# RWKV-7 attention and a SoLU block: couplings with 33 weight columns from chunk 12 on, the second block's inverse loaded into place, the first coupling ahead of two waves of h

## The chip, the cores and the metric

The kernel runs on one core of a Trainium2 chip. The time is device microseconds of one execution, the median of several runs. An engine has its own instruction queue: PE (TensorE) multiplies matrices into PSUM, PEld is its loading of weights, DVE (VectorE) and ACT (ScalarE) work on tiles, POOL (GpSimd) does a little arithmetic and issues DMAs, SP issues DMAs only. A queue runs in order, so an instruction that waits holds up everything behind it on its engine.

## The reference

Two blocks in a row. The first is a recurrence over 768 steps for 4 batches of 8 heads, with a state of 40 x 40 each:

```python
for t in range(S):
    y[:, :, t] = np.einsum('bhd,bhde->bhe', rt, state)
    Sa = np.einsum('bhde,bhe->bhd', state, at)
    state_decay = state * wt[:, :, None, :] - np.einsum('bhd,bhe->bhde', Sa, bt)
    state = state_decay + np.einsum('bhd,bhe->bhde', vt, kt)
```

Its output, as 3072 tokens of 320, goes through the second: h = x @ w_in (320 to 1024), e = exp(h - max), solu = h * e / sum(e), a normalization over the 1024 columns, and a product with w_out back to 320.

## The kernel before, in words

The 768 steps are cut into chunks of C = 64 tokens, and two batches share the 128 partitions, so there are 24 pieces of work (12 chunks of the sequence for 2 pairs of batches), called chunk 0 to 23 below. Within a chunk the recurrence becomes matrix products, with one triangular system of 64 unknowns for each of 16 pairs of batch and head. The inverse of its matrix is made in blocks of Q = 32: DVE inverts the two 32 x 32 diagonal blocks, for two chunks at once (`invert`, L543), and SP stores them to DRAM as `uu_dram` (`unloaded`, L566). `bring` (L573) loads them back in two shapes: the first block into `tu`, columns Q to 2Q, the second into the lower rows of `uh`. Then two couplings on PE make the block below the diagonal, and put it beside the second block:

- `flip` (L586), on DVE, transposes the first block inside `tu`.
- `couple` (L592), the first coupling: 16 matmuls of `nt` (weights, 64 rows x 64 columns) with the flipped first block (32 moving columns), into the PSUM tile `py`. ACT copies the result to `wy` (L602), times a mask `hi` that clears the upper 32 rows of each half. The right half of `wy` holds a constant, the identity in the lower rows.
- `close` (L605), the second coupling: 16 matmuls of `wy` (64 x 64) with `uh` (32 moving columns). The product gives the block below the diagonal in the upper rows, and, through the identity in `wy`, the second block itself in the lower rows. ACT copies all of it to the last third of `tu` (L614), "tu's tail" below.
- `solved` (L730), a step of the loop later, multiplies `tu` with `x0`.

The 16 matmuls of a coupling take turns over four tiles of 64 x 64 of the array (`in_turn`, L309); `mm` is the helper at L317, so that all of them carry the line L318. The weights' columns become the result's partitions.

The main loop (L1149) runs over i. Step i works on several chunks at once: it prepares chunk i + 5, couples chunk i + 1, solves chunk i, and does the second block's h for chunk c = i - 2. The second block's product h is cut into five waves (`hidden`, L814; 18 matmuls of 512 moving columns and 4 of 256 in all), and `run` (L1236) places them between the other PE work by the table `waves` (L1233): from i = 5 to 22 two go at place 2, one at place 3, one at place 6 (L1293), just ahead of the first coupling, and one at place 7 (L1298), between the two couplings. The second coupling is at L1300, `driven` (`px<-lv,psi`) at L1303.

Every operation is recorded under a name by `do` and then emitted in the order of the list `ORDER` (L31); names that the list does not hold follow in the order in which they were recorded. The list ends with the work around the coupling of chunk 10, so from chunk 11 on the loop's own order stands. At the end of step i the queues get, in this order: `rs` (POOL, L871), the loads of `tu` and `uh` for chunk i + 2 (`bring_`, L1338; SP), the stores of x for chunk i (`leave`, L796; POOL, three DMAs, read back by SP at L812 as `xT`), and at the start of an odd step the load of r for a later chunk (L371; POOL), which ACT copies in the same step (`by_value`, L379). In even steps the inverse of the next two chunks has been stored (L570, SP) just before.

Of the kernel before, what the change touches and what calls it, by code (L numbers as in the profile page):

```python
# [13 lines left out]
AF = mybir.ActivationFunctionType  # L14
# [3 lines left out]
P = 128  # L18
C = 64
Q = 32  # L20
# [7 lines left out]
SPLITS = {2: (0, 0, 0, 2, 4), 24: (0, 0, 0, 0, 2)}  # L28


ORDER = """  # L31
w0 b0 b1 w1 a0 lg0 Tc0 xi0 xe0 Tei0 sb0 Tb0 Ta0 L1 lg1 Tc1 Eei0 Ea0 v0 Eb0 xi1 xe1 N0 nt0 Tei1 Eei1 sb1 Tb1 a1 Ta1 Ea1
L0 Eb1 N1 nt1 w2 lg2 a2 Tc2 nb0 k0 Z0 sn0 nb1 ns1 nf1 sn1q sk0 ns0 nf0 sn1 w3 xe2 b2 Z1 Ta2 xi2 B0 Tei2 Eei2 r0 Ea2
# [65 lines left out]
def kernel(  # L99
# [18 lines left out]
    nc = tc.nc  # L118
    B, H, S, D = r.shape
# [24 lines left out]
    def c_(name):  # L144
        lo, hi = where[name]
        return cst[:, lo:hi]
# [22 lines left out]
    for x in ex_t:  # L169
# [8 lines left out]
    wy = const.tile([P, 2, 4, C], FP32, name="wy")  # L178
    nc.vector.tensor_copy(out=wy.rearrange("p h j c -> p (h j) c")[:, :, Q:],
                          in_=c_("eye_hi").unsqueeze(1).to_broadcast([P, 8, Q]))  # L180
# [114 lines left out]
    def centred(mean):  # L295
        for x in range(0, NF, NF // 2):
            nc.vector.tensor_tensor(out=w2[:, x:x + NF // 2], in0=w2[:, x:x + NF // 2],
                                    in1=mean.unsqueeze(1).to_broadcast([P, NF // 2, DM]), op=ALU.subtract)


    def half(p):
        return slice(C * p, C * p + C)
# [6 lines left out]
    def in_turn(tile_of, some=units):  # L309

        lots = {}
        for u in some:
            lots.setdefault(tile_of(*u), []).append(u)
        lots = list(lots.values())
        return [lot[n] for n in range(max(map(len, lots))) for lot in lots if n < len(lot)]

    def mm(o, lhsT, rhs, start=True, stop=True):  # L317
        nc.tensor.matmul(o, lhsT=lhsT, rhs=rhs, start=start, stop=stop, skip_group_check=True)  # L318
# [28 lines left out]
    def ok(i):  # L347
        return 0 <= i < N
# [145 lines left out]
    def shared_pair(i):  # L494

        if i not in shared:
            shared[i] = pair(st[i]["Y"], "py")
        return shared[i]
# [74 lines left out]
    def bring(i, which):  # L573
        if not ok(i):
            return
        d = st[i]
        d["tu"], d["uh"] = tu_t[i % 2], uh_t[i % 2]
        n, at = divmod(i, GRP)
        src = inverse[n].rearrange("c (e a x h) t -> e a c x h t", e=2, a=GRP, x=2)
        for x in range(2 * (which == "t")):  # L580
            queue = nc.sync if i or not x else nc.gpsimd
            queue.dma_start(out=d["tu"][C * x:C * x + Q, :, Q:2 * Q], in_=src[0, at, :, x])
        for x in range(2 * (which == "u")):
            nc.sync.dma_start(out=d["uh"][C * x + Q:C * x + C], in_=src[1, at].rearrange("c x h t -> c (x h) t"))

    def flip(i):  # L586
        if not ok(i):
# [4 lines left out]
    def couple(i):  # L592
        if not ok(i):
            return lambda: None
        d = st[i]
        t = shared_pair(i)
        for u in in_turn(lambda p, q, g, h: (p ^ h, p)):
            p, q, g, h = u
            j = 2 * q + g
            x = half(p ^ h)  # L600
            mm(t[half(p), h, j * Q:j * Q + Q], d["nt"][x, p, j], d["tu"][x, 4 * p + j, 0:Q])
        return lambda: nc.scalar.activation(out=wy[:, :, :, 0:Q], in_=t[:, :, 0:4 * Q].rearrange("p h (j c) -> p h j c", j=4),  # L602
                             func=AF.Copy, scale=c_("hi"))

    def close(i):  # L605
        if not ok(i):
            return lambda: None
        d = st[i]
        t = shared_pair(i)
        for u in in_turn(lambda p, q, g, h: (p, p ^ h)):  # L610
            p, q, g, h = u
            j = 2 * q + g
            mm(t[half(p ^ h), p, 384 + j * Q:384 + j * Q + Q], wy[half(p), h, j], d["uh"][half(p), H * (p ^ h) + 4 * p + j])
        return lambda: nc.scalar.copy(out=d["tu"].rearrange("p (h j) c -> p h j c", h=2)[:, :, :, 2 * Q:],  # L614
                       in_=t[:, :, 384:].rearrange("p h (j c) -> p h j c", j=4))


    def attend_kv(i, t, which):
# [322 lines left out]
    def do(name, fn, *args):  # L941
        seq.append((name, lambda: fn(*args)))

    def do_pe(name, fn):
        box = []
        do(name, lambda: box.append(fn()))
        return box
# [25 lines left out]
    def vector(plan, i=None):  # L973
        for word in plan.split():
            if word in "bsf":
                stage = "bsf".index(word)
                x = begun[stage]
                begun[stage] += 1
                do(f"n{word}{x}", narrowed, x, stage)
                if stage == 2 and x in LANDS_NEXT:  # L980
                    do(f"L{LANDS_NEXT[x]}", land, LANDS_NEXT[x], nc.gpsimd)
            else:
                some(int(word.strip("o")), (i + 2) // GRP if "o" in word else N)
# [29 lines left out]
    def evict(name, box, *which):  # L1013
        if which:
            do(name, lambda: [box[0][x]() for x in which])
        else:
            do(name, lambda: box[0]())
# [22 lines left out]
    def bring_(i):  # L1040
        if ok(i):
            do(f"tu{i}", bring, i, "t")
            do(f"uh{i}", bring, i, "u")

    def xy(i):
        return "BC" if i < EARLY - AHEAD else ("BC", "CB")[(i - EARLY + AHEAD) % 2]
# [89 lines left out]
    reads(1)  # L1136
    scaled_(4, "k")
    bring_(0)
    bring_(1)
    do("L3", land, 3, nc.sync)  # L1140
    keys(5, "k")
# [7 lines left out]
    for i in range(-1, N + LAG + 1):  # L1149
        j, c = i + AHEAD, i - LAG  # L1150
# [85 lines left out]
        def run(x):  # L1236
            if not ok(c):
                return
            for _ in range(waves[x]):
                n = next(wave)  # L1240
                do(f"H{c}.{n}", hidden, c, n)
            if sum(waves[:x + 1]) == NK and sum(waves[:x]) < NK:
                do(f"m{c}", highest, c)
# [46 lines left out]
        ahead = 2 + (i >= EARLY - AHEAD)  # L1290
        logged_(j + ahead)
        vector(plan[2], i)
        run(6)  # L1293
        if ok(i + 1):
            evict(f"wy{i + 1}", do_pe(f"C{i + 1}", lambda i=i: couple(i + 1)))
        if i == LAG + 1:
            do("centre", lambda: centred(mean["mean2"]))
        run(7)  # L1298
        if ok(i + 1):
            evict(f"tl{i + 1}", do_pe(f"D{i + 1}", lambda i=i: close(i + 1)))  # L1300
# [31 lines left out]
        if i >= 0:  # L1332
            some(Q, (i + 2) // GRP)
            odd = steady and i % GRP == 1
            if odd:
                keys(j + 2, "k")
                keys(j + 4, "w")
            bring_(i + 2)  # L1338
            if odd:
                keys(j + 3, "ak")  # L1340
                keys(j + 5, "w")
# [21 lines left out]

    place = {name: x for x, name in enumerate(ORDER.split())}
    for name, piece in sorted(seq, key=lambda x: place.get(x[0], len(place))):
# [31 lines left out]
```

## Time and profile before

| what | value |
|---|---|
| median of 3 runs | 532.44 us (528.31 to 536.37) |
| the profiled execution | 535.16 us, span 533.3 us |
| mean granted TensorE clock | 0.990 |
| PE busy | 487.6 us, 91% of the span |
| DVE, ACT, POOL busy | 420.0, 313.1, 180.2 us |
| first and last coupling | 60.5 us, 486.7 us |

The span is from the first to the last instruction of the program. Lines of the profile are read as: source line, engine, operation, output<-inputs, for matmuls "rows*columns" of weights and the shape of the moving operand, and xN for the number of records. A matmul in fp32 is recorded as two passes, so 16 matmuls are x32. "SPq" is SP's queue of DMA issues. Where a wait is given, it reads "idle time <- what ended it".

### The profile page before, as it was taken

The page shows a single profiled execution, that of the slowest core. Times are in us where ns is not written, and L with a number is a line of the kernel's source. Part 1 is how long each engine was busy: PE and PEld are TensorE (multiplying, and loading weights), DVE is VectorE, ACT ScalarE, POOL GpSimd, SP SyncE. Part 2 cuts the span into 40 slices and gives each one's busy share as a digit, 9 for nine tenths or more (in the row PEclk, how much of TensorE's full clock was granted, in tenths as well). Part 3 has the DMA queues.
Part 4 walks back from the last instruction along what each step waited for, and adds up shares of the span by engine and source line. Part 5 has one row for each costly group of instructions (what it writes and reads, how often), then busy time and mean ns, then how long its engine had stood idle before and what let it go on. Part 6 is the DMA issues. An engine that isn't in the chain of part 4 may idle for free.

```text
span 533.3 us, 28056 instructions
## 1 busy us (share of the span) xinstructions
PE 487.6 (91%) x12029; PEld 394.7 (74%) x12029; DVE 420.0 (79%) x1800; ACT 313.1 (59%) x627; POOL 180.2 (34%) x328
## 2 busy tenths in 40 slices
PE   4457589898999999999999999999999999999997
PEld 3345476666888877877888788788778877887766
DVE  5589988998998988879789879879979888544322
ACT  3546457785856655745766665566556655664433
POOL 3543237224434242533053343334252421210300
PEclk9999988998999999999999999999999999999999
DMA  9997679846666778766266675676554551420210
GB/s 155 171 185 149 150 140 187 189 95 118 133 134 129 131 154 142 150 142 141 48 135 117 124 163 100 116 152 123 105 120 95 109 115 43 103 68 27 62 53 25
DMA packets 194475, 63.95 MB, mean 120 GB/s; under 512 B 166840, under 2 KB 186528, under 8 KB 194352
## 3 DMA queue, kind: packets, MB, share of 16 engines
q1 hardware_dynamic: 181232, 41.60, 42.3%
q0 software_dynamic: 10768, 19.95, 15.8%
q8 instruction: 94, 1.54, 1.3%
q10 hardware_dynamic: 2352, 0.62, 0.7%
q14 instruction: 29, 0.24, 0.1%
HBM read 47.96 MB, written 14.16 MB: 116 GB/s over the span
## 4 chain that ended last, share of the span: by engine, by line
PE 77%; DMA 8%; DVE 7%; ACT 3%; SPq 3%; issue 2%; DVEq 0%; ACTq 0%
PE po L318 19%; PE h L318 18%; PE py L318 6%; PE pyo L318 6%; PE px L318 6%; PE ps L318 4%; PE pu L318 3%; DMA a<-in_a_dram 3%; PE plnT L883 2%; PE pkv L435 2%; PE psr L318 2%; PE pb L435 2%; PE pa L435 2%; SPq L344 2%; DVE prod L560 1%
## 5 line engine op out<-in xcount | busy, mean ns | idle before, releaser
L318 PE MATMUL h<-w_in,xT 64*64 64x512 f32 (+1 forms) x1064 | 122.2, 551 | 0.4 <-issue 0.2
L318 PE MATMUL po<-w,lnT 128*128 128x160 f32 x768 | 114.7, 304 | 0.0
L318 PEld LDWEIGHTS po<-w,lnT 128*128 128x128 f32 x768 | 105.4, 190 | 4.6 <-issue 0.8
L560 DVE TENSOR_TENSOR prod<-blk,uu 128x48 f32<-128x48 f32 (+19 forms) x576 | 93.9, 204 | 1.2
L563 DVE TENSOR_TENSOR uu<-uu,prod 128x48 f32<-128x48 f32 (+19 forms) x576 | 94.2, 204 | 0.0
L525 POOL DMA_DIRECT2D nt_dram<-nt x86 | 50.1, 590 | 110.9 <-ACT nt L513 109.6
L318 PEld LDWEIGHTS h<-w_in,xT 64*64 64x64 f32 x1064 | 38.9, 133 | 24.9 <-issue 20.6
L834 DVE TENSOR_REDUCE nmax<-h 128x1 f32<-128x1024 f32 x24 | 29.3, 1221 | 32.1 <-PE h L318 31.5
L871 POOL TENSOR_TENSOR rs<-var,mhalf 128x1 f32<-128x1 f32 x24 | 13.7, 571 | 119.4 <-ACT var L863 119.1
L344 POOL DMA_DIRECT2D raw_r<-in_r_dram x48 | 33.0, 692 | 26.5 <-ACT r L379 24.5
L862 ACT ACTIVATE sq<-e,mu 128x1024 f32<-128x1024 f32 x24 | 26.9, 1120 | 19.9 <-DVE e L850 19.9
L479 DVE TENSOR_TENSOR lu<-pu,cst 128x512 f32<-128x512 f32 x24 | 16.5, 687 | 27.0 <-PE pu L318 27.0
L842 ACT ACTIVATE e<-h,nmax 128x1024 f32<-128x1024 f32 x24 | 26.7, 1110 | 17.5 <-DVE nmax L834 17.3
L850 DVE SCALAR_TENSOR_TENSOR e<-h,e 128x1024 f32<-128x1024 f32 x24 | 29.3, 1221 | 5.4 <-ACT e L842 5.2
L602 ACT ACTIVATE wy<-py,cst 128x256 f32<-128x256 f32 x24 | 11.4, 474 | 37.4 <-PE py L318 37.4
L802 POOL DMA_DIRECT2D x_dram<-x x24 | 18.0, 750 | 37.9 <-DVE x L793 37.7
L552 DVE SCALAR_TENSOR_TENSOR uu<-blk,uu 128x30 f32<-128x30 f32 (+3 forms) x144 | 26.9, 242 | 2.5 <-DMA blk<-nt_dram 1.9
L665 ACT COPY st<-psr 128x416 f32<-128x416 f32 (+1 forms) x44 | 14.2, 377 | 24.7 <-PE psr L318 24.7
L629 ACT COPY kvT<-pkv 104x1024 f32<-104x1024 f32 x24 | 24.2, 1010 | 6.7 <-PE pkv L435 6.4
L318 PEld LDWEIGHTS py<-tu,nt 64*64 64x64 f32 x768 | 16.3, 141 | 14.2 <-issue 7.6
L318 PE MATMUL pu<-x,tu 64*64 64x104 f32 x768 | 25.9, 265 | 0.7 <-ACT bT L445 0.5
L318 PE MATMUL px<-lv,psi 64*64 64x104 f32 x768 | 24.2, 264 | 2.2 <-DVE lv L479 2.2
(154 smaller groups left out, 1067.5 us busy)
## 6 DMA issues: line engine op xcount, KB each, us to landing
xT<-x_dram SPq DMA_DIRECT2D x48, 160.0 KB, 3.9
blk<-nt_dram POOLq DMA_DIRECT2D x22, 256.0 KB, 4.8
raw_w<-in_w_dram SPq DMA_DIRECT2D x48, 80.0 KB, 3.7
lv<-in_v_dram SPq DMA_DIRECT2D x48, 80.0 KB, 3.1
raw_r<-in_r_dram POOLq DMA_DIRECT2D x48, 80.0 KB, 3.6
out_dram<-osb SPq DMA_DIRECT2D x46, 80.0 KB, 3.8
a<-in_a_dram SPq DMA_DIRECT2D x44, 80.0 KB, 3.7
raw_k<-in_k_dram SPq DMA_DIRECT2D x42, 80.0 KB, 3.4
```

The lines of the kernel that those rows point to most:

```text
L318: nc.tensor.matmul(o, lhsT=lhsT, rhs=rhs, start=start, stop=stop, skip_group_check=True)
L344: queue.dma_start(out=x[half(p), :, 0:D], in_=ap[2 * bp + p, :, ci * C:(ci + 1) * C, :].rearrange("h t d -> t h d"))
L435: nc.tensor.transpose(out=t[0:W2, p, at + C * j:at + C * j + C], in_=x[half(p), 2 * j:2 * j + 2].rearrange("p a b -> p (a b)")[:, skip:ski ...
L525: queue.dma_start(out=blocks[n][e].rearrange("(a x h) s c -> a x s h c", a=GRP, x=2)[at, x], in_=nt[home:home + Q].rearrange("p h j c -> p ...
L552: nc.vector.scalar_tensor_tensor(out=u[:, c, j + 1:Q], in0=nb[:, j, j + 1:Q], scalar=u[:, c, j:j + 1], in1=u[:, c, j + 1:Q], op0=ALU.mult, ...
L560: nc.vector.tensor_tensor(out=ts[-1], in0=nb[:, j:j + 1, j + 1:Q].to_broadcast([P, hi - lo, m]), in1=u[:, lo:hi, j:j + 1].to_broadcast([P, ...
L563: nc.vector.tensor_tensor(out=u[:, lo:hi, j + 1:Q], in0=u[:, lo:hi, j + 1:Q], in1=x, op=ALU.add)
L629: return lambda: nc.scalar.copy(out=o[0:W2].rearrange("p b j t -> p b (j t)"), in_=t[0:W2])
L834: nc.vector.tensor_reduce(out=nmax, in_=d["h"], axis=AX.X, op=ALU.max, negate=True)
L842: nc.scalar.activation(out=e, in_=d["h"], func=AF.Exp, bias=d["nmax"], accum_out=d["esum"])
L850: nc.vector.scalar_tensor_tensor(out=d["e"], in0=d["h"], scalar=1.0 / DFF, in1=d["e"], op0=ALU.mult, op1=ALU.mult, accum_out=d["mu"])
L862: nc.scalar.activation(out=pair("A" if i == N - 2 else "h", "sq").rearrange("p a b -> p (a b)"), in_=d["e"], func=AF.Square, scale=-float( ...
```

## The change

For chunks 12 to 23 (`i < NARROWED` keeps the old way for the others):

- The first coupling loads only the last 33 columns of `nt` as weights, so its result has 33 rows; two ACT copies, one for each half of the partitions, put them in `wy`, without the mask.
- `uh` holds the second block in rows 1 to 32 of each half (row 0 stays zero), and only the 8 of 16 slots that the half needs.
- The second coupling loads 33 rows and 33 columns of `wy`. Two ACT copies of 32 rows each bring the upper rows into `tu`.
- The second block comes into the lower rows of `tu`'s last third by two new DMAs on POOL (`ut`), recorded right behind the loads of `tu` and `uh`.
- The wave at place 6 is emitted behind the first coupling, so that both waves stand between the couplings.

```diff
+NARROW = Q + 1
+NARROWED = 12
...
         for x in range(2 * (which == "u")):
-            nc.sync.dma_start(out=d["uh"][C * x + Q:C * x + C], in_=src[1, at].rearrange("c x h t -> c (x h) t"))
+            if i < NARROWED:
+                nc.sync.dma_start(out=d["uh"][C * x + Q:C * x + C], in_=src[1, at].rearrange("c x h t -> c (x h) t"))
+            else:
+                nc.sync.dma_start(out=d["uh"][C * x + 1:C * x + 1 + Q, 0:H].rearrange("c (x h) t -> c x h t", x=2),
+                                  in_=src[1, at][:, :, 4 * x:4 * x + 4])
+        for x in range(2 * (which == "v")):
+            nc.gpsimd.dma_start(out=d["tu"][C * x + Q:C * x + C, :, 2 * Q:], in_=src[1, at, :, x])
...
-            mm(t[half(p), h, j * Q:j * Q + Q], d["nt"][x, p, j], d["tu"][x, 4 * p + j, 0:Q])
-        return lambda: nc.scalar.activation(out=wy[:, :, :, 0:Q], in_=t[:, :, 0:4 * Q].rearrange("p h (j c) -> p h j c", j=4),
-                             func=AF.Copy, scale=c_("hi"))
+            if i < NARROWED:
+                mm(t[half(p), h, j * Q:j * Q + Q], d["nt"][x, p, j], d["tu"][x, 4 * p + j, 0:Q])
+            else:
+                mm(t[C * p:C * p + NARROW, h, j * Q:j * Q + Q], d["nt"][x, p, j, C - NARROW:], d["tu"][x, 4 * p + j, 0:Q])
+
+        def evict():
+            if i < NARROWED:
+                nc.scalar.activation(out=wy[:, :, :, 0:Q], in_=t[:, :, 0:4 * Q].rearrange("p h (j c) -> p h j c", j=4),
+                                     func=AF.Copy, scale=c_("hi"))
+                return
+            for p in range(2):
+                at = slice(C * p, C * p + NARROW)
+                nc.scalar.copy(out=wy[at, :, :, 0:Q], in_=t[at, :, 0:4 * Q].rearrange("p h (j c) -> p h j c", j=4))
+        return evict
...
-            mm(t[half(p ^ h), p, 384 + j * Q:384 + j * Q + Q], wy[half(p), h, j], d["uh"][half(p), H * (p ^ h) + 4 * p + j])
-        return lambda: nc.scalar.copy(out=d["tu"].rearrange("p (h j) c -> p h j c", h=2)[:, :, :, 2 * Q:],
-                       in_=t[:, :, 384:].rearrange("p h (j c) -> p h j c", j=4))
+            y, z = p ^ h, slice(C * p, C * p + NARROW)
+            if i < NARROWED:
+                mm(t[half(y), p, 384 + j * Q:384 + j * Q + Q], wy[half(p), h, j], d["uh"][half(p), H * y + 4 * p + j])
+            else:
+                mm(t[C * y:C * y + NARROW, p, 384 + j * Q:384 + j * Q + Q], wy[z, h, j, 0:NARROW], d["uh"][z, 4 * y + j])
+
+        def evict():
+            for y in range(1 if i < NARROWED else 2):
+                at = slice(0, P) if i < NARROWED else slice(C * y, C * y + Q)
+                nc.scalar.copy(out=d["tu"][at].rearrange("p (h j) c -> p h j c", h=2)[:, :, :, 2 * Q:],
+                               in_=t[at, :, 384:].rearrange("p h (j c) -> p h j c", j=4))
+        return evict
...
             do(f"uh{i}", bring, i, "u")
+            if i >= NARROWED:
+                do(f"ut{i}", bring, i, "v")
...
-        run(6)
+        if i + 1 < NARROWED:
+            run(6)
         if ok(i + 1):
             evict(f"wy{i + 1}", do_pe(f"C{i + 1}", lambda i=i: couple(i + 1)))
+        if i + 1 >= NARROWED:
+            run(6)
```

## The prediction, as it stands on record

> **What bounds the kernel now.** I read the page first: busy time, then the chain that ended last, then the stretch in which the changed chunks run, and at last one step of it, engine by engine.
>
> ```profile
> span 533.3 us, 28056 instructions
> PE 487.6 (91%) x12029; PEld 394.7 (74%) x12029; DVE 420.0 (79%) x1800; ACT 313.1 (59%) x627; POOL 180.2 (34%) x328
> PE 77%; DMA 8%; DVE 7%; ACT 3%; SPq 3%; issue 2%; DVEq 0%; ACTq 0%
> raw_r<-in_r_dram POOLq DMA_DIRECT2D x48, 80.0 KB, 3.6
> ```
>
> The table by stretch, for the part in which chunks 12 to 23 are coupled (columns: length, then busy time of PE, PEld, DVE, ACT, POOL, granted clock, DMA share, GB/s):
>
> ```profile
> 285.00:490.00 205.00, 203.90 (x5520) 166.96 (x5513) 163.19 (x711) 123.57 (x244) 65.75 (x112) 1.00 0.52 107
> ```
>
> PE is busy for 203.9 of 205.0 us, at full clock; DVE, ACT and POOL have 20% and more to spare. In this stretch time is saved only where PE's own work gets shorter, and lost only where PE is made to wait. One step of it, in PE's order (start, length, operation, count):
>
> ```profile
> 312.94 0.39 PE L435 MATMUL pkv<-cst,kb 64*104 64x64 f32 x8
> 313.16 0.39 PE L435 MATMUL pkv<-cst,v 64*104 64x64 f32 x8
> ...
> 314.76 0.71 PE L883 MATMUL plnT<-cst,e 64*128 64x64 f32 x16
> 315.31 0.39 PE L435 MATMUL pst<-cst,st 64*104 64x64 f32 x8
> ...
> 320.03 0.65 PE L318 MATMUL psr<-rT,s 40*64 40x64 f32 x32
> 320.49 1.04 PE L318 MATMUL h<-w_in,xT 64*64 64x512 f32 x8
> ...
> 321.82 0.90 PE L318 MATMUL px<-st,aT 40*64 40x104 f32 x32
> 322.54 0.90 PE L318 MATMUL pyo<-lv,kb 64*64 64x104 f32 x32
> 323.25 1.04 PE L318 MATMUL h<-w_in,xT 64*64 64x512 f32 x8
> 324.11 0.62 PE L318 MATMUL py<-tu,nt 64*64 64x32 f32 x32
> 324.55 1.07 PE L318 MATMUL h<-w_in,xT 64*64 64x512 f32 x12
> 325.44 0.62 PE L318 MATMUL py<-uh,wy 64*64 64x32 f32 x32
> 325.88 0.92 PE L318 MATMUL px<-lv,psi 64*64 64x104 f32 x32
> ```
>
> A length holds the drain of the last matmul, so the price of a group is from its start to the next group's start. The first coupling (py<-tu,nt) costs 0.44 us, the second (py<-uh,wy) 0.44 us, the waves of h between them 0.86 and 0.89 us. Each of the 16 matmuls of a coupling is recorded as two passes, and four tiles of 64x64 take turns, so a tile makes 8 passes, one every 55 ns.
>
> **Part 1: 33 weight columns in place of 64, in both couplings.** A pass has a load of weights and a stream of moving columns. With 64 moving columns (psr) 32 passes cost 0.46 us, 57 ns each in its tile; with 104 (px<-st) 0.72 us, 90 ns. 40 columns more cost 33 ns, or 0.8 ns each, so 32 columns would stream in 26 ns. The couplings take 55 ns: what holds them is not the moving side, but the 64 weight columns or a floor under any pass. The transposes tell which: with 104 weight columns 8 passes on two tiles cost 0.22 us, 55 ns in a tile; with 128, 16 cost 0.55 us, 69 ns, at the same 64 moving columns. So weight columns do cost time where they are the longer side: 14 ns for 24 of them, 0.6 ns each. No row has a pass with 33. By that slope a pass gets 18 ns shorter; in proportion to the columns (55 x 33/64 = 28) it gets 27 ns shorter, which just reaches the 26 ns of the stream. The last pass of a tile is still followed by a load of 64 columns, so 7 passes of 8 gain: 0.13 to 0.19 us for a coupling. I take 0.16, between them, since the shape of the tile is that of the couplings but the slope is that of transposes. Two couplings in 12 chunks: 24 x 0.16 = 3.8 us less, all of it on PE and so on the path. The ends are 0 (a floor) and 24 x 0.19 = 4.6 us; a loss is the third rival.
>
> On the floor: the Trainium skill, "TensorEngine Tiling (Array Packing)", section Performance Considerations, says that each matmul carries about 60 cycles of overhead, so that one with a free size of 1 takes as long as one of 60. By that rule 32 and 64 moving columns cost the same whatever the weights are, which is what 0.44 and 0.46 us show, and this part would save nothing; the transposes' 55 and 69 ns speak for the weights. It is the first rival.
>
> **Part 2: the first coupling ahead of both waves.** It now starts where the wave at 323.25 did, 0.86 us earlier. What it needs is there: DVE's flip of tu ended at 321.27, and ACT's copy out of the same bank (nt) at 322.68.
>
> ```profile
> 320.83 0.44 DVE L590 STREAM_TRANSPOSE tu<-tu 128x256 f32<-128x256 f32 x1
> ```
>
> ```profile
> 322.08 0.60 ACT L513 ACTIVATE nt<-py 128x512 f32<-128x512 f32 x1 [0.68 <-PE py L318]
> 322.58 0.45 ACT L379 COPY v<-lv 128x320 f32<-128x320 f32 x1
> 322.93 0.46 ACT L379 COPY r<-raw_r 128x320 f32<-128x320 f32 x1
> 323.29 0.47 ACT L384 ACTIVATE lw<-raw_w 128x320 f32<-128x320 f32 x1
> 324.81 0.47 ACT L602 ACTIVATE wy<-py,cst 128x256 f32<-128x256 f32 x1 [1.06 <-PE py L318]
> 326.14 0.37 ACT L614 COPY tu<-py 128x256 f32<-128x256 f32 x1 [0.85 <-PE py L318]
> 326.88 0.86 ACT L728 ACTIVATE x<-px 128x832 f32<-128x832 f32 x1 [0.37 <-PE px L318]
> ```
>
> What it removes is the second coupling's wait for wy:
>
> ```profile
> PEld py L318 <- ACT wy L602: 2.1, 12, 0.2
> ```
>
> 2.1 us in 12 waits is the weight loader's time. The matmuls behind it hardly wait: the wave before them takes 0.89 us, the other wave 0.86, so at most 0.03 us a chunk, 0.4 us in all. I take 0.
>
> **Part 3: two copies for wy and two for tu's tail, in place of one each.** ACT starts equal copies about 0.35 us apart (322.58, 322.93), so a pair takes about 0.3 + 0.37 = 0.67 us where wy took 0.47 and the tail 0.37. With part 2, PE ends the first coupling at 323.25 + 0.28 = 323.53; ACT begins 0.26 later, as it did (324.55 to 324.81), at 323.79, and has both halves at 324.46. The second coupling is due after two waves, at 323.53 + 1.75 = 325.28. The cover is 0.8 us; without it the 0.2 us longer pair would stand on the path 12 times, 2.4 us. The tail has ACT's 0.37 us of idle time before x behind it, which holds the 0.3 more. Nothing on the path.
>
> **Part 4: the second block's inverse.** Its two loads into uh stay on SP as two issues (0.91 us) and, by the shapes in the diff, bring half the bytes in pieces of 512 B where they were of 2 KB; they land long before the coupling 9 us later: nothing. New are two loads into tu on POOL, placed behind rs and ahead of the three stores of x and the loads of r:
>
> ```profile
> 313.38 0.56 POOL L871 TENSOR_TENSOR rs<-var,mhalf 128x1 f32<-128x1 f32 x1 [3.23 <-ACT var L863]
> 313.96 0.76 POOL L802 DMA_DIRECT2D x_dram<-x  x1
> ...
> 315.84 1.40 POOL L344 DMA_DIRECT2D raw_r<-in_r_dram  x2
> 322.97 2.31 POOL L525 DMA_DIRECT2D nt_dram<-nt  x4 [5.74 <-ACT nt L513]
> ```
>
> ```profile
> 310.05 1.32 SPq L570 DMA_DIRECT2D uu_dram<-uu  x2
> 315.79 0.81 SPq L582 DMA_DIRECT2D tu<-uu_dram  x2
> 316.66 0.91 SPq L584 DMA_DIRECT2D uh<-uu_dram  x2
> ...
> 325.02 1.24 SPq L812 DMA_DIRECT2D xT<-x_dram  x2
> ```
>
> A POOL load of these 128-byte pieces costs 2.31/4 = 0.58 us to issue, so 1.16 us a chunk in POOL's 5.7 us of idle time. The cost is in the wait: in every even chunk the inverse has only just been stored, and SP's own load of it started at 315.79, while POOL was free at 313.94. So POOL stands until 315.79, stores x from 316.95 to 318.83 and loads r from there, 3.0 us later than now. xT, due at 325.02, does not feel it. The r copy on ACT does: the second load is issued near 319.5 and lands 3.6 us later (median), at 323.1, and ACT's copy began at 322.93. 0.2 us late, against a cover of 0.8: nothing. Two chunks on, the store took longer:
>
> ```profile
> 348.28 3.77 SPq L570 DMA_DIRECT2D uu_dram<-uu  x2
> 354.99 0.82 SPq L582 DMA_DIRECT2D tu<-uu_dram  x2
> ```
>
> ```profile
> 360.31 0.46 ACT L379 COPY r<-raw_r 128x320 f32<-128x320 f32 x1
> ```
>
> There r would be issued from 354.99 + 1.16 + 1.88 = 358.03, the second near 358.7, and land at 362.3, 2.0 us after ACT wants it. lw and wy stand behind it on ACT, and the second coupling would wait 2.0 - 0.8 = 1.2 us. I take one such wait in the six even chunks, 1.0 us; the ends are 0 and 6 x 1.2 = 7.2 us.
>
> **The sum.** -3.8 + 0 + 0 + 1.0 = -2.8 us: the span from 533.3 to 530.5, the profiled execution from 535.16 to 532.4. That execution lies 2.7 us above the median of the runs (532.44, from 528.31 to 536.37), so the median goes to 529.6.
>
> **The rivals.** First, the floor: 55 ns is what any pass takes, and narrower weights save nothing; then +1.0 remains, 533.4. For it: 32 and 64 moving columns cost alike. Against it: the transposes. Second, and slower: POOL's wait. Each even chunk stores its inverse late enough that r lands over 0.8 us after ACT wants it, which is where it decides. At 1.2 us in all six and the 3.8 saved it gives 532.44 + 7.2 - 3.8 = 535.8. For it: 354.99. Against it: the chunk at 315.79, which stays under the cover. Third, the narrow tiles no longer run four abreast: a coupling goes from 0.44 to 0.88 us and the kernel to 532.44 + 24 x 0.44 + 1.0 = 544.0. Against it: 33 columns and 33 rows still need a tile of 64, in the same turns.
>
> **How the numbers follow.** My forecast has a chance of 0.55, the floor 0.17, POOL's wait 0.20, tiles no longer abreast 0.05; 0.03 is left for a gain beyond 4.6 us. The forecast alone runs from 527.4 (all 4.6 and the 0.4 of part 2 saved, no wait) to 532.4 (3.0 saved by the slope, three waits of 1.0). The range reaches out by the scatter of the runs on the low side and to POOL's rival on the high side: 525.5 to 536.0. A measurement tells about 2%, 10.6 us, from no change. All PE time of the 24 couplings is 24 x 0.44 = 10.6 us, so faster by over 2% is nearly out, 0.02; slower by over 2% is the third rival and a little more, 0.06; the rest, 0.92, lies within.
>
> **What would show it.** In the profile after, a coupling's start to the next group's start: near 0.28 us confirms part 1, 0.44 is the floor, 0.88 the third rival. The second coupling should no longer be waiting for wy, with both waves ahead of it. On POOL the loads into tu wait for uu_dram in even chunks; ACT's r copy with a wait for raw_r, and PE idle before the second coupling, would show the second rival. I am wrong if PE idles elsewhere in this stretch, or if a coupling's price lies outside 0.25 to 0.44 us.

## The result, and the profile after

The kernel after takes 534.69 us (median of 20 runs, 532.38 to 542.95), the kernel before 533.38 us in the same series (20 runs, 527.6 to 541.27): a ratio of 1.0075, 95% interval 1.0052 to 1.0098. The ratios, here and below, leave out the runs that took over 1.5% longer than the fastest of their kernel (three of the 20 after, up to five of twelve below), and the medians of all 20 lie only 1.3 us apart. By the ratio it is some 4 us slower, less than the 2% that the prediction set as its bound for a difference, and on the other side than its 529.6 us. The two profiled executions alone would mislead: 535.16 us before, 534.15 us after.

The page after; first the head of it, then the chain's shares and the loads of r:

```profile
span 532.4 us, 28157 instructions
PE 483.4 (91%) x12029; PEld 391.9 (74%) x12029; DVE 420.1 (79%) x1800; ACT 320.5 (60%) x651; POOL 194.3 (36%) x352
...
PE 65%; DVE 13%; DMA 9%; SPq 6%; ACT 3%; issue 3%; POOL 1%; DVEq 0%; POOLq 0%; ACTq 0%
...
raw_r<-in_r_dram POOLq DMA_DIRECT2D x48, 80.0 KB, 4.0
```

PE is busy for 4.2 us less, but its share of the chain falls from 77% to 65%, and DVE (7% to 13%), SP's queue (3% to 6%), DMA and POOL gain. The shares are of the whole span, and part of that lies ahead of the change. The stretch in which chunks 12 to 23 are coupled, by the same table as in the prediction:

```profile
285.00:490.00 205.00, 201.10 (x5439) 164.65 (x5432) 162.33 (x696) 129.42 (x264) 77.34 (x132) 1.00 0.52 107
```

PE now idles 3.9 of 205 us where it idled 1.1, and POOL has 11.6 us more to do. To measure the stretch itself I take the start of `px<-lv,psi` in chunk 11 and in chunk 23 (first before, then after):

```profile
270.13 0.47 PE L318 MATMUL px<-lv,psi 64*64 64x104 f32 x12
...
486.81 0.48 PE L318 MATMUL px<-lv,psi 64*64 64x104 f32 x12
```

```profile
268.02 0.47 PE L320 MATMUL px<-lv,psi 64*64 64x104 f32 x12
...
485.80 0.30 PE L320 MATMUL px<-lv,psi 64*64 64x104 f32 x1
```

216.7 us before, 217.8 after. What lies ahead of it (270.1 and 268.0 us) isn't touched by the change, and what lies behind is 46.5 us in both. In the profiles of all kernels below the part ahead lies anywhere from 263 to 274 us; that scatter is why a whole time says little about 3 us, and why the stretch is followed instead.

A step without trouble, chunk 14's, in PE's order:

```profile
320.97 0.46 PE L320 MATMUL py<-tu,nt 64*33 64x32 f32 x31
...
321.26 1.96 PE L320 MATMUL h<-w_in,xT 64*64 64x512 f32 x19
323.00 0.49 PE L320 MATMUL py<-uh,wy 33*33 33x32 f32 x31
323.31 0.30 PE L320 MATMUL px<-lv,psi 64*64 64x104 f32 x1
```

The first coupling costs 0.29 us (0.27 to the first pass of the waves, which is among the lines left out), the second 0.31, where each cost 0.44. Two chunks on, in chunk 16:

```profile
358.17 0.47 PE L320 MATMUL py<-tu,nt 64*33 64x32 f32 x31
...
358.47 1.96 PE L320 MATMUL h<-w_in,xT 64*64 64x512 f32 x19
362.36 0.46 PE L320 MATMUL py<-uh,wy 33*33 33x32 f32 x32 [1.92 <-ACT wy L621]
```

The two waves take 1.74 us in chunk 14, so here they are done at 360.2, and PE then stands for about 2 us. ACT, SP's queue and POOL's queue at that time tell why:

```profile
357.49 0.45 ACT L381 COPY v<-lv 128x320 f32<-128x320 f32 x1
360.84 0.46 ACT L381 COPY r<-raw_r 128x320 f32<-128x320 f32 x1 [2.90 <-DMA raw_r<-in_r_dram]
361.20 0.47 ACT L386 ACTIVATE lw<-raw_w 128x320 f32<-128x320 f32 x1
361.57 0.73 ACT L621 COPY wy<-py 33x256 f32<-33x256 f32 x2
```

```profile
346.61 3.16 SPq L572 DMA_DIRECT2D uu_dram<-uu  x2
353.18 1.71 SPq L584 DMA_DIRECT2D tu<-uu_dram  x2
```

```profile
348.30 0.56 POOL L899 TENSOR_TENSOR rs<-var,mhalf 128x1 f32<-128x1 f32 x1 [3.71 <-ACT var L891]
353.73 1.23 POOL L592 DMA_DIRECT2D tu<-uu_dram  x2 [4.87 <-PE ps L320]
354.95 0.71 POOL L830 DMA_DIRECT2D x_dram<-x  x1
...
356.77 1.39 POOL L346 DMA_DIRECT2D raw_r<-in_r_dram  x2
```

Read it from the bottom. POOL is free at 348.86 but its next instruction, `ut`, waits for the stored inverse. The row names PE as the releaser, yet SP's load of the same inverse starts at 353.18 and `ut` at 353.73: by that, both wait for the landing of `uu_dram`. The stores of x and the loads of r stand behind `ut`, r is issued at 356.77, and ACT's copy waits 2.9 us for it. The copies of w and `wy` stand behind that one, and PE behind `wy`. No wait of that copy for `raw_r` is in the stretch before.

In chunk 18, where PE waits 0.85 us for `wy`, the chain that ended last runs through each of these links by name, from the store of the inverse to the second coupling (start, length, what):

```profile
384.01 6.66 DMA uu_dram<-uu
...
391.27 1.23 POOL tu L592 x2
...
394.31 0.70 POOL raw_r L346
395.02 3.64 DMA raw_r<-in_r_dram
...
398.68 0.46 ACT r L381
399.14 0.27 ACT wy L621
...
399.84 0.46 PE py L320 x32
```

### The profile page after: what moved, and what is told of

It is laid out like the page before. It is cut to its first block, busy times and chain, and to the rows that moved or that the text cites. A ratio compares the mean times of both kernels' runs of the same rounds, so it can differ in the third digit from the quotient of the medians.

```text
span 532.4 us, 28157 instructions
## 1 busy us (share of the span) xinstructions
PE 483.4 (91%) x12029; PEld 391.9 (74%) x12029; DVE 420.1 (79%) x1800; ACT 320.5 (60%) x651; POOL 194.3 (36%) x352
## 3 DMA queue, kind: packets, MB, share of 16 engines
q8 instruction: 94, 1.54, 1.2%
## 4 chain that ended last, share of the span: by engine, by line
PE 65%; DVE 13%; DMA 9%; SPq 6%; ACT 3%; issue 3%; POOL 1%; DVEq 0%; POOLq 0%; ACTq 0%
PE po L320 18%; PE h L320 15%; PE pyo L320 5%; PE px L320 5%; PE py L320 4%; SPq L346 4%; DVE prod L562 3%; PE pu L320 3%; PE ps L320 3%; DVE uu L565 3%; PE plnT L911 2%; DMA uu_dram<-uu 2%; PE psr L320 2%; PE pkv L437 1%; PE pa L437 1%
## 5 line engine op out<-in xcount | busy, mean ns | idle before, releaser
L320 PEld LDWEIGHTS h<-w_in,xT 64*64 64x64 f32 x1064 | 41.4, 133 | 32.5 <-issue 27.9
L890 ACT ACTIVATE sq<-e,mu 128x1024 f32<-128x1024 f32 x24 | 26.9, 1119 | 20.6 <-DVE e L878 20.5
L641 ACT COPY tu<-py 32x256 f32<-32x256 f32 (+1 forms) x36 | 13.2, 365 | 29.9 <-PE py L320 29.8
L554 DVE SCALAR_TENSOR_TENSOR uu<-blk,uu 128x30 f32<-128x30 f32 (+3 forms) x144 | 26.9, 242 | 3.1 <-DMA blk<-nt_dram 2.5
L799 DVE TENSOR_TENSOR tot<-pyo,st 104x416 f32<-104x416 f32 x44 | 24.2, 583 | 5.4 <-PE pyo L320 5.3
```

Source lines behind the costliest of these rows:

```text
L554: nc.vector.scalar_tensor_tensor(out=u[:, c, j + 1:Q], in0=nb[:, j, j + 1:Q], scalar=u[:, c, j:j + 1], in1=u[:, c, j + 1:Q], op0=ALU.mult, ...
L799: nc.vector.tensor_tensor(out=by_b(d["tot"])[:, :, :, part], in0=answers(i)[:, :, :, part], in1=by_b(state_of(i)[:, x])[:, :, :, 0:HW], op ...
L890: nc.scalar.activation(out=pair("A" if i == N - 2 else "h", "sq").rearrange("p a b -> p (a b)"), in_=d["e"], func=AF.Square, scale=-float( ...
```

## The experiments

"Stretch" is chunk 11's to chunk 23's `px<-lv,psi` in the profile, and in brackets chunks 12 to 19 and 20 to 23. The ratio is to the kernel before in the same series. Each stretch is that of one profiled execution.

| kernel | stretch, us | ratio, 95% interval |
|---|---|---|
| before | 216.7 (148.8, 67.8) | |
| after | 217.8 (149.6, 68.2) | 1.0075 (1.0052 to 1.0098) |
| e1_sp | 216.2 (146.5, 69.7) | 0.9973 (0.9936 to 1.0011) |
| e2_late | 214.3 (146.2, 68.1) | 0.9991 (0.9957 to 1.0025) |
| e3_load | 219.9 (151.5, 68.4) | 1.0025 (0.9981 to 1.0069) |
| e4_cr | 214.2 (146.1, 68.2) | 0.9988 (0.9952 to 1.0025) |
| e5_after | 217.3 (150.1, 67.2) | 1.0035 (0.9997 to 1.0072) |
| e6_late_nomove | 215.6 (146.8, 68.9) | 0.9961 (0.9930 to 0.9992) |
| e7_move | 217.2 (148.7, 68.5) | 1.0009 (0.9976 to 1.0042) |
| e8_late_cr | 214.9 (146.7, 68.2) | 0.9992 (0.9944 to 1.0039) |
| e9_before | 216.9 (149.0, 67.8) | 1.0010 (0.9963 to 1.0057) |
| e10_early | 214.5 (146.4, 68.1) | 1.0040 (1.0009 to 1.0072) |
| e11_n32 | 217.1 (148.4, 68.6) | 1.0039 (0.9994 to 1.0083) |
| e12_n48 | 217.1 (147.3, 69.9) | 1.0009 (0.9971 to 1.0047) |
| e13_even | 216.7 (148.9, 67.8) | 1.0019 (0.9985 to 1.0054) |
| e14_odd | 214.3 (145.8, 68.6) | 0.9958 (0.9925 to 0.9990) |
| e15_late | 214.9 (146.1, 68.8) | 1.0013 (0.9975 to 1.0052) |
| e16_late_nomove | 214.5 (146.5, 68.0) | 1.0012 (0.9974 to 1.0049) |
| e17_load_late | 216.1 (147.1, 69.0) | 1.0051 (1.0015 to 1.0088) |
| e18_pairs | 215.5 (147.6, 67.9) | 1.0026 (0.9993 to 1.0060) |

**Where `ut` stands: e1, e2, e13, e14.** e1 issues it on SP, e2 on POOL behind the loads of r:

```diff
-            nc.gpsimd.dma_start(out=d["tu"][C * x + Q:C * x + C, :, 2 * Q:], in_=src[1, at, :, x])
+            nc.sync.dma_start(out=d["tu"][C * x + Q:C * x + C, :, 2 * Q:], in_=src[1, at, :, x])
```

```diff
-            if i >= NARROWED:
-                do(f"ut{i}", bring, i, "v")
...
+        if ok(i + 1) and i + 1 >= NARROWED:
+            do(f"ut{i + 1}", bring, i + 1, "v")
```

> The kernel after, with the two loads of the second block into tu (ut) issued by SP, right behind uh, in place of POOL. Theory: the 5 us that the narrow couplings' 3.6 us were lost to are POOL's wait for the stored inverse, which makes r late, and with it ACT's copies of r, w and wy, in the even chunks. Then the r copy no longer waits for raw_r, and the time is that of the kernel before less about 3.6 us, up to 0.5 us back for two more issues on SP: 530 (ratio to before 0.993 to 0.995). Rival 1, the loss is ACT's pairs of copies or the moved wave: nothing changes, 534.7, ratio 1.007. Rival 2, the loss is the 24 additional transfers themselves, on the DMA engines: also 1.007.

> The kernel after, with ut still on POOL, but recorded behind the loads of r at the start of the next step. POOL issues as many DMAs as in the kernel after, but nothing that is urgent stands behind them. Theory (POOL's wait ahead of r): as with SP, about 530, ratio 0.993 to 0.995. Rival, POOL's time for the two issues (1.2 us a chunk): 534 to 535, ratio about 1.006, since the issues are still there. Rival, the transfers themselves or ACT's pairs: 1.007.

In both, no wait of ACT for `raw_r` and none of PE for `wy` is left. Chunk 16's step, 20.3 us after, takes 18.7 and 18.5. The stretch falls to 216.2 and 214.3; chunks 12 to 19 take 146.5 and 146.2 us where they took 149.6. So neither ACT's pairs nor the transfers are what chunks 12 to 19 lost. The whole times fall less than was expected, to about that of the kernel before (0.9973 and 0.9991 for 0.993 to 0.995). e13 and e14 put `ut` on POOL in every other chunk, on SP in the rest (`nc.sync if i % GRP else nc.gpsimd` in e13, the two swapped in e14):

> The kernel after, with ut on POOL in the even chunks alone (12, 14, ... 22), and on SP in the odd ones. Theory (POOL waits for the inverse that has just been stored, which is so in even chunks alone): all of the loss stays, the stretch from chunk 11 to 23 takes 217 to 218 us, ratio 1.002 to 1.008. Rival (POOL's two issues in every chunk are what costs): half of it, about 215.8.

> The mirror of e13_even: ut on POOL in the odd chunks alone, on SP in the even ones. Theory: none of the loss stays, no wait of ACT's r copy for raw_r, stretch 214 to 216 us, ratio 0.994 to 0.998. Rival (POOL's issues): half of it, about 215.8, with the steps of odd chunks 0.3 us or more longer than 18.2 and 16.7.

With the even chunks on POOL the loss comes back, this time in chunk 14, whose step takes 21.2 us. The stretch, 216.7 us, lies between the two forecasts; the step and the waits tell which holds. Waits in e13 from 268 to 490 us, of ACT, PE and POOL (us in all, times, the longest):

```profile
ACT r L381 <- DMA raw_r<-in_r_dram: 7.0, 5, 3.4
```

```profile
PE py L320 <- ACT wy L621: 2.4, 1, 2.4
```

```profile
POOL tu L592 <- DMA uu_dram<-uu: 5.6, 1, 5.6
```

With the odd chunks on POOL there are no such waits, and PE idles 0.76 of the 205 us:

```profile
285.00:490.00 205.00, 204.24 (x5502) 168.28 (x5496) 161.56 (x692) 131.93 (x267) 73.21 (x125) 1.00 0.51 107
```

The loss hangs on the even chunks, where the inverse has just been stored, and not on POOL's issues.

**The load alone, and r behind wy: e3, e4, e8.** e3 adds `ut` alone to the kernel before, at the place that it has after:

```diff
...
             do(f"uh{i}", bring, i, "u")
+            if i >= 12:
+                do(f"ut{i}", bring, i, "v")
```

> The kernel before, with wide couplings, one wave at its old place and single ACT copies, plus the two POOL loads of ut alone at the place where the kernel after has them (tu's tail overwrites them with the same values). Theory: the loads alone cost what the kernel after lost, about 5 us: 538, ratio 1.008 to 1.011. Since the second coupling has only one wave of cover for wy here, it may be more: up to 1.015. Rival, ACT's pairs or the moved wave: 533.4, ratio 1.000 to 1.002.

The stretch takes 219.9 us, 3.2 more than before, with a stall of PE in chunk 16 that is named by the same row: `PE py L318 <- ACT wy L605: 2.3, 1, 2.3`. Chunk 16's step is 2.6 us longer than before (21.14 for 18.55), so most of it is there. The load alone does it. The ratio of 1.0025 is below the 1.008 to 1.011 that was expected; over all twelve runs the median is 533.0 us beside 528.5.

e4 leaves POOL as it is after, and records the copy of r behind `wy`:

```diff
-            do(f"cr{i}", by_value, i, "r")
...
             evict(f"wy{i + 1}", do_pe(f"C{i + 1}", lambda i=i: couple(i + 1)))
+        if ok(i + 2) and i + 2 > NARROWED:
+            do(f"cr{i + 2}", by_value, i + 2, "r")
```

> The kernel after, with POOL's order unchanged, but ACT's copy of r (chunks 13 on) recorded behind the copy of the first coupling (wy). r is as late as in the kernel after, but wy and the copy lw no longer stand behind it on ACT. Theory: PE's wait before the second coupling goes; what r feeds is not due before the next step, so most of the 5 us come back: 530 to 531.5, ratio 0.993 to 0.997. If r itself is what PE waits for: 534.7, ratio 1.007.

r still comes late (ACT waits 2.2 us in all for it, in three places), but nothing that PE needs stands behind it: 214.2 us. So the last link, ACT's order, is shown too. e8 makes both edits, e2's and e4's:

> Experiments e2 and e4 together: ut behind the loads of r, and ACT's copy of r behind wy. If each took away the same stalls of the even chunks, both together give no more than either: stretch 214 to 214.5 us, ratio 0.994 to 0.999. If r still holds up wy at times in e2 (as it does in the kernel before), they add up: 213.5 us or less, that is 12 steps of 18.2, 18.2, 18.2, 18.2, 18.2, 18.2, 18.2, 17.5 and four of 16.7.

214.9 us: they take away the same stalls, and don't add up.

**The kernel after and the kernel before again: e5, e9.**

> The kernel after once more, unchanged, in one series with the three below. In the first four experiments the kernel before took 528.5 us, 5 us less than in the series in which it stood against the kernel after, so the two series can't be read against each other without it. Theory: POOL's wait costs more than the narrow couplings save, whatever the level: ratio 1.004 to 1.010, and from chunk 11's px<-lv,psi to chunk 23's again 217 to 218.5 us (before 216.7), with a stall of over 1 us in chunk 16. Rival: the 1.0075 came from the stretch ahead of the change, which differs from run to run by 4 us in the profiles: then 0.993 to 1.002 here.

The stretch is at 217.3 us, with stalls in chunks 12 and 16 (20.3 us each, 18.2 without). PE's waits and ACT's:

```profile
PE py L320 <- ACT wy L621: 4.6, 4, 2.0
```

```profile
ACT r L381 <- DMA raw_r<-in_r_dram: 11.7, 6, 2.9
```

> The kernel before against itself, for two things: how far two sets of runs of one kernel lie apart, and a second profile of its stretch from chunk 11's px<-lv,psi to chunk 23's. Expected: ratio 0.997 to 1.003, stretch 215.3 (no stall in any step) to 217 us; the first profile had 216.7. If the stretch is at 215 or below here, the 2.4 us that e2 and e4 gained on it are partly the first profile's own stalls.

The two stretches of the kernel before differ by 0.2 us, those of the kernel after by 0.5, those of e2's edit (e2, e15) by 0.6. But the whole time of one kernel against itself comes with an interval of half a per cent to each side.

**The move and the pairs: e6, e7, e15, e16, e18.** e7 is the kernel before with the moved wave alone; e6 and e16 are e2 with the wave back ahead of the first coupling; e15 is e2 again; e18 is e7 with ACT's copies in pairs of 64 partitions for wide couplings.

```diff
-        run(6)
+        if i + 1 < 12:
+            run(6)
         if ok(i + 1):
             evict(f"wy{i + 1}", do_pe(f"C{i + 1}", lambda i=i: couple(i + 1)))
+        if i + 1 >= 12:
+            run(6)
```

> The kernel before with the move of the wave alone, from chunk 12 on: wide couplings, single copies, no ut. Prediction's part 2: 0 to 0.4 us less, the stretch at 216.3 to 216.7 us, ratio 0.999 to 1.000. Rival, the move itself costs (the first coupling is then due 0.86 us earlier, and waits for the flip of tu or for the copy of nt): over 217.5 us in the stretch, ratio over 1.002.

> Experiment e2 (ut behind the loads of r) with the wave at place 6 put back ahead of the first coupling, so that only one wave, 0.86 us, stands between the couplings. Two ACT copies end about 0.26 + 0.74 = 1.0 us after the first coupling. Theory of the prediction (the move is the cover for the pair): PE waits 0.15 to 0.3 us for wy in each of 12 chunks, 2 to 3.6 us, so the stretch from chunk 11 to 23 takes 216 to 218 us where e2 took 214.3, ratio 0.999 to 1.005. Rival, the pair is hidden by one wave: 214.3, as e2.

> Experiment e2 once more (ut behind the loads of r, with the move), in one series with the next: stretch 214 to 215 us, ratio 0.994 to 0.999.

> Experiment e6 once more (without the move). Its steps without a stall were 0.12 us longer than those of e2 (18.30 against 18.18, 16.82 against 16.70), 1.4 us in twelve, by PE's wait for the second half of wy: stretch 215.3 to 216 us, ratio 0.3% above e15. Rival, from the whole times so far (0.9961 against 0.9991): the move costs, and this version lies 0.3% under e15.

> The kernel before with the moved wave and with ACT's copies in pairs (64 partitions each) for wy and tu's tail from chunk 12 on; couplings wide, no ut. Prediction's part 3: the pairs cost nothing behind two waves: ratio 0.998 to 1.002, stretch 216.3 to 217.2 us, no wait of PE or the weight loader for wy. If the pairs hold up ACT elsewhere, or if the stops come with them, the stretch is at 217.5 or above, with chunk 20's step at 17.3 or more.

e7's steps without a stop (18.46 to 18.55 us) are those of the kernel before: the move by itself is worth nothing. Without it the narrow version's steps are 0.12 us longer in each chunk (18.30 and 18.18, 16.82 and 16.70), by the weight loader's wait in e16:

```profile
PEld py L320 <- ACT wy L621: 4.8, 12, 0.4
```

That is 1.4 us in twelve, near the scatter of one stretch (e6 215.6, e16 214.5) and under that of the whole times: e6's 0.9961 was not repeated by e16. The pairs (e18) cost nothing: 215.5 us, and no wait for `wy`.

**More narrow chunks: e10.** e2 with `NARROWED = 8`, and `ut8` to `ut11` in the list behind the stores of x (`ut8` ahead of the next loads of r, where no wait is recorded).

> Experiment e2 with four more chunks narrow, 8 to 11, whose ut stands on POOL behind the stores of x and the loads of r as well. By part 1 (0.29 us in place of 0.44 for a coupling) 8 more couplings save 1.2 us, all on PE, which is busy for over 94% of the time from 100 us on: ratio to before 0.992 to 0.997, and the step of chunk 11 0.3 us shorter. Rival: these steps are not set by PE's own work, and nothing is gained over e2: 0.995 to 0.999.

The rival was right: the steps of chunks 10 and 11 take 19.30 and 17.67 us (19.04 and 17.76 before). In this profile PE's own work doesn't set these steps, and the ratio, 1.0040, is above the 0.992 to 0.999 that both expected.

**The price of a weight column: e11, e12.** e2 with `NARROW = 32` and `NARROW = 48`, and `uh`'s block in rows `NARROW - Q` to `NARROW`.

> Experiment e2 with 32 weight columns in place of 33 (uh's block in rows 0 to 31). If the price of a pass is the columns of its weights, one column less changes nothing: 0.28 to 0.29 us for a coupling, 33 ns for a pass of a tile, stretch as e2's 214.3. Third rival of the prediction, brought nearer: with 32 columns and 32 rows a smaller tile is chosen, and the four tiles no longer run abreast or take turns otherwise: 0.44 to 0.9 us for a coupling, stretch 216 to 229 us.

> Experiment e2 with 48 weight columns (16 rows of zeros above uh's block), to measure what a weight column costs. Passes of a tile take 33 ns with 33 columns and 58 ns with 64, 0.8 ns for each column. By that line 48 columns give 45 ns, 0.36 us for a coupling, and of 3.6 us half is left. If the pass is held by something else that jumps at 33 or at 64, it stays at 33 ns (0.29 us) or at 58 ns (0.44 us).

The first coupling of chunk 21 in e2 (33 columns), e12 (48) and e11 (32), on PE:

```profile
442.07 0.90 PE L320 MATMUL pyo<-lv,kb 64*64 64x104 f32 x32
442.79 0.46 PE L320 MATMUL py<-tu,nt 64*33 64x32 f32 x31
443.06 0.64 PE L320 MATMUL h<-w_in,xT 64*64 64x512 f32 x1
```

```profile
444.84 0.52 PE L320 MATMUL py<-tu,nt 64*48 64x32 f32 x32
445.18 1.07 PE L320 MATMUL h<-w_in,xT 64*64 64x512 f32 x8
```

```profile
443.79 0.90 PE L320 MATMUL pyo<-lv,kb 64*64 64x104 f32 x32
444.61 0.46 PE L320 MATMUL py<-tu,nt 64*32 64x32 f32 x32
445.00 1.52 PE L320 MATMUL h<-w_in,xT 64*64 64x512 f32 x14
```

0.27 us with 33 columns and 0.34 with 48, where 64 cost 0.44. In the median the passes of one tile follow each other every 33, 45 and 58 ns: 0.8 ns a column, as e12's line had it. With 32 columns a pass takes 32 ns, and yet the coupling takes 0.39 us and the group ahead of it 0.82 us, where both together take 0.99 in e2: PE pauses by 0.10 to 0.15 us more at each of the four borders between a coupling and its neighbours. All steps are 0.4 us longer than in e2 (18.6 and 17.1 us), and the whole gain is gone. The Trainium skill, "TensorEngine Tiling (Array Packing)", section Key Properties, says that a change of the tiling mode drains TensorE. The pauses of e11 fit that; the trace doesn't show the mode itself.

**The load late in the wide kernel: e17.** The kernel before with e2's `ut`.

> The kernel before with the two POOL loads of ut at the harmless place of e2, behind the loads of r; tu's tail overwrites them with the same values. Theory: POOL's issues and the transfers cost nothing by themselves: ratio 0.998 to 1.002, stretch 216.3 to 217 us. If the stops in chunks 20 to 23 come with the transfers, chunk 20's step is 17.3 us or more where the kernel before takes 16.97, and the stretch is at 217.5 or above.

Of the stretch the load costs nothing (216.1 us), and no wait for `raw_r` is there. The whole time, 1.0051, says otherwise, and that isn't explained (below).

## Why the prediction was wrong

**Part 1 was right in the price of a coupling.** A coupling costs 0.29 to 0.31 us for a forecast of 0.28. The steps that nothing disturbs are 0.26 to 0.36 us shorter (18.18 for 18.46, 17.49 for 17.85, 16.70 for 16.96), 0.32 was forecast. The rivals of the floor and of tiles no longer abreast are out. With 32 columns, too, a pass takes 32 ns; what that one column costs are the pauses at the borders. The rule that stood for the floor, some 60 cycles for any matmul (the Trainium skill, "TensorEngine Tiling (Array Packing)", Performance Considerations), is not what held these passes: with 32 moving columns as before, they went from 58 to 33 ns.

**Parts 2 and 3 were right.** e7 and e18 show no cost, and e6 and e16 a worth of 0.12 us a chunk for the cover.

**Part 4 failed**, at the sentence "I take one such wait in the six even chunks, 1.0 us". The mechanism was the one described, link by link: e3 and e13 bring the loss back with `ut` alone or in the even chunks alone, e1, e2, e4 and e14 take it away. Its size was not: PE's recorded waits for `wy` are 2.8 us in the kernel after and 4.6 in its second profile, in two and four places, and the stretch is 2.7 us longer than without them: 217.6 (mean of the two) beside 214.8 (mean of e1, e2, e4, e8, e14, e15). The cover of 0.8 us was nearly right: in chunk 16 ACT was 2.9 us late, and PE stood for 1.9. The error was to take the landing of the inverse from one execution as if it were a property of the chunk. SP's load of it, counted from the `px<-lv,psi` of the chunk before, starts for chunk 16 after 10.3 us in the profile before and after 7.9 us in e9, which is the same kernel; over all profiles after 7.9 to 12.4 us for chunk 16, and after 7.9 to 11.7 for chunk 14. The stall goes with it: chunk 16 after and in e3, 12 and 16 in e5, 14 in e13, with 0.9 and 0.6 us more in chunk 18 after and in e5. Chunk 14, put aside because its `uu_dram` was there at 315.79, is where e13 loses most. So the second rival, "POOL's wait", is what happened, at about 2 us in one or two chunks in place of 1.2 in six.

The times of the profile before were also not those of the kernel after: for chunk 18 the load starts after 6.3 to 8.4 us in the four wide profiles without `ut`, and after 8.3 to 9.9 in the 16 with it. Why is not shown.

**The gain did not arrive whole either.** The step of Part 1 that failed is "all of it on PE and so on the path". Without the wait the stretch is 1.7 us shorter than in the wide kernels without `ut` (214.8 beside 216.6, mean of before, e7, e9, e18; the profiles of either group scatter by 2 us), where 24 couplings at 0.14 us less make 3.4. So the sum for the stretch, forecast as -3.8 + 1.0 = -2.8 us, came out near -1.7 + 2.7 = +1.0. Chunks 12 to 19 give 2.3 us, all that their 16 couplings have to give; chunks 20 to 23, where 1.1 us was due, come out 0.6 us longer. There PE stops in the middle of a group, as in the kernel after in chunk 20's step (17.84 us where 16.7 is the rule):

```profile
427.38 2.58 PE L320 MATMUL h<-w_in,xT 64*64 64x512 f32 x15
429.32 0.44 PE L320 MATMUL psr<-rT,s 40*64 40x64 f32 x8
429.80 0.59 PE L320 MATMUL h<-w_in,xT 64*64 64x512 f32 x1
```

Two waves are 16 passes, four abreast every 0.43 us, and take 1.72 us (445.22 to 446.94 in chunk 21). Here only three start at 428.24 and at 428.67; the last two passes come alone, at 429.32, after a pause of 0.63 us, and at 429.80, though no wait is recorded. The table of DMA queues for the 0.3 us from 426.4 on has this line (packets, MB, share of 16 engines):

```profile
q8 instruction: 1, 0.02, 26.9%
```

26.9% of 16 x 0.3 us is 1.29 us: a load of 16 KB of instructions that starts at about 426.5 and ends at 427.8, 1.5 us ahead of the end of the pause. This queue moves 94 such packets in the kernel before, 1.54 MB, which is 64 bytes for each of the 24058 matmuls and weight loads. In the stretches of all profiles PE stands idle 33 times by more than 0.12 us between two matmuls of one group without a recorded releaser, and all 33 times it goes on 1.2 to 1.8 us after the end of such a packet, while the packets come 4.7 us apart there. (The pause above is not among them: the profile models when a matmul ends, and counts next to no idle time there.) That fits PE waiting for its instructions; no run changed when they come, so it is argued, not shown. Wide kernels have these pauses too (3 in each profile of the kernel before, 0.7 to 0.8 us in all); where they fall is not the same from one execution to the next. What brings them to chunks 20 to 23 is open. None of the four wide profiles without `ut` has one there, and the two wide kernels with `ut`, e3 and e17, have one each, which speaks for the additional loads rather than for the narrow couplings; e17's chunks 20 to 23 are 1.2 us longer than before, e18's are not, in one profile each.

**What stays open.** The six versions without the wait have whole times of 0.9986 on the mean, 0.7 us under the kernel before, where their stretch says 1.7; the kernel after lies 4 and 1.9 us above it in its two series, where the stretch says 1.0 and 0.6 (and the medians of all runs 1.3 and 0.1). e10 and e17, at 1.0040 and 1.0051, have nothing in their profiles to show for it. Either something in unprofiled executions costs another 1 to 3 us, or the intervals are too narrow for a part ahead of the change that scatters by 10 us; these runs can't tell. e14 has the best ratio, 0.9958 (0.9925 to 0.9990), 0.8 to 1.2% under the kernel after in its two series; that it beats the kernel before too rests on this one interval.

## What to carry to other kernels

A DMA issue that waits for data holds up every issue behind it on its queue: before a load is put on a queue, look at what stands behind it there, who copies that, and what stands behind the copy. A time at which a transfer lands in one profile is a sample; a plan that lives on 1 us of slack behind it should hold for a landing 2 us later, or stand where nothing waits behind it. Where the gain is less than the scatter of whole runs, measure the changed stretch between two marks of the trace, in more than one profile.

## What the runs showed of the hardware

- With 32 moving columns a matmul was held by its weights: 33, 48 and 64 weight columns gave 0.27, 0.34 and 0.44 us for 32 passes, and 33, 45 and 58 ns from pass to pass of a tile, 0.8 ns a column. The Trainium skill, "TensorE: Matmul & The Clock Gate", section LDWEIGHTS (loading the stationary operand), gives columns divided by 1.2 in ns, 0.83 a column. The slope agrees; the passes here take some 5 ns more than that.
- One weight column less, 32 for 33, left a pass at 32 ns and cost 0.4 us a step, through pauses of 0.10 to 0.15 us at the four borders between groups.
- Packets of 16 KB on the queue that the profile calls instruction take about 1.1 us each. PE's pauses in the middle of a group end 1.2 to 1.8 us behind one of them; the profile shows them as no wait at all or as "issue" (0.49 us at 342.13 in the kernel after).
